# Layer norm of the later tokens with the features on the partitions, in the head of an attention and MLP kernel

## The chip, the cores and the metric

One core of a Trainium2 chip. The metric is the device time of one execution in microseconds (us); several runs are given by their median. Engines: PE is the matrix engine (PEld its weight loads), DVE, ACT and POOL are the vector, scalar and GpSimd engines, SP is SyncE, which issues transfers. Each engine works through its own queue in order and waits on semaphores.

## The reference

2048 tokens of 512 features, float32. The head of the kernel, which is what changes, computes the layer norm and the projections q, k, v.

```
xn = (x - mean(x)) / sqrt(var(x) + 1e-5)              # over the 512 features
q, k, v = split(xn @ wqkv)                            # 32 heads of 16
s = softmax(q k^T / 4) v, heads joined, @ wo
h = relu(xn @ w1 + b1)^2 @ w2 + b2                    # 1792 hidden
out = x + s * silu(h)
```

## The kernel before

Products are made to near float32 accuracy from a high and a low part: every operand `t` is split into `hi` (float32r) and `lo = t - hi`, and a product is three matmuls (hi hi, hi lo, lo hi). With four blocks of 128 features (`KO`) a projection tile of 128 x 512 is twelve matmuls.

**The head**, in program order on PE, ACT, DVE and POOL (`manual_schedule`), works on 16 token tiles of 128 tokens with the tokens on the partitions:
- `load_x` brings a tile, `ln_stats` its mean and variance (DVE) and root (ACT), `ln_norm` scales it (ACT, the first two on DVE).
- `ln_high` turns it on PE: four 128x128 transposes into a `pm` bank of PSUM. ACT copies the bank to the high part of `xTs[c]` (chunk `c` of 512 tokens, features on the partitions), `ln_low` (DVE) subtracts for the low part.
- Between these steps `pump(n)` puts the next `n` projection matmuls into PE's queue: K tiles `("qk", 4, c)`, Q tiles `("qk", 0, c)` and value tiles `("v", c, tt)`. `qk_done` copies a bank to `raw`, POOL splits it into `hl` (`split`) and `qk_store` writes it to DRAM (`q_d`, `k_d`); `v_done` copies a value bank to one of seven `vt` buffers and stores it to `v_d`.
- Weights: `raw_m` and `raw_v` are split into `wa_t` (first Q and K columns, and values). `raw_r`, in the buffer `wv`, is loaded twice, once in the head and once in round 0 of the lead, for the two halves of `wr_t` (the other Q and K columns).
- `spill` writes finished chunks of `xTs` to `xn_d` for the MLP; two more copies keep 256 tokens of chunk 0 in the tile `ka3`; `b1_t` and `b2_t` are loaded.
- When all of K of the first heads is in `k_d`, `load_k` reads it back into two tiles `ka`: twelve transfers of 16 partitions, each a whole row of 2048 keys. `load_q` does the same for Q.

SP's order in the head is left to the scheduler, which places a transfer by its own priorities; from the lead on it is the program's (`lead.enter_context(...)`).

**The lead rounds** follow. Two lanes of 64 rows of PE run side by side; each round a lane issues a matmul of a side tile (the remaining projections, `side_rounds`) and now and then a maximum over 512 keys (`max_mm`, L401 on PE and L408 on DVE), which reads `ka`. Side tiles take the banks `pm`, `pm`, `pd`, `pm`, ... in turn, with three `pm` buffers, and ACT empties a bank when both lanes are done. After the maxima of round group 3 the second half of `wr_t` is split (`split_w`: ACT high parts, POOL low parts):

```
            if g == 0:
                raw_r = [load_w("wv", 3 * P, KO * (5 * P + D))]
            if g == 3:
                for ko in range(KO):
                    split_w(wr_t, ko, slice(3 * P, 6 * P), raw_r[0][:, ko])
```

Lines in the profile: transposes L1394; Q and K tiles of the head L1207, value tiles L1273; side tiles L1303; `raw` and `vt` copies L1224 and L1282; weight copies on ACT L1136; spills L1458; the copies into `ka3` L1538, the biases L1542 and L1545; `load_k` L181, `load_q` L170, weight loads L1145.

Of the kernel before, what the change touches and what calls it, by code (L numbers as in the profile page):

```python
# [73 lines left out]
def kernel(  # L74
    ctx: ExitStack,
    tc: tile.TileContext,
    x: bass.AP,
    wqkv: bass.AP,
# [18 lines left out]
    sp_d = dram.tile([S, D], F32, name="sp_d")  # L97
    xn_d = dram.tile([2, P, KO, S], F32, name="xn_d")
# [33 lines left out]
    with ExitStack() as ph:  # L132
# [42 lines left out]
        def load_k(qd, n):  # L175

            p, j, i = n // 6, n // 3 % 2, n % 3
            if n % 6 == 0:
                kas[qd, p] = ring("ka")
            h = 4 * qd + 2 * p + j  # L180
            nc.sync.dma_start(  # L181
                kas[qd, p][64 * j + DH * i : 64 * j + DH * (i + 1), :].bitcast(F32),
                k_d[h // 8][i % 2, (h % 8) * DH : (h % 8 + 1) * DH, :],
            )
# [13 lines left out]

        def load_q(u, name):
            tiles = []  # L200
            for p in range(2):
                load_q_pair(u, name, p, tiles)
            return tiles
# [928 lines left out]
        def split_w(dst, kos, cols, raw, pool=False):  # L1132
            if pool:
                split((dst[:, 0, kos, cols], dst[:, 1, kos, cols]), raw)
                return
            nc.scalar.activation(dst[:, 0, kos, cols], raw, AF.Copy)  # L1136
            nc.gpsimd.tensor_tensor(
                dst[:, 1, kos, cols], raw, dst[:, 0, kos, cols].bitcast(F32), op=ALU.subtract
            )

        def load_w(name, width, at, kos=(KO,)):
            raw = st.tile([P, KO, width], F32, name=name)
            k0 = 0
            for n in kos:
                nc.sync.dma_start(  # L1145
                    raw[:, k0 : k0 + n],
                    wqkv[:, at + k0 * width : at + (k0 + n) * width].rearrange(
                        "p (k n) -> p k n", n=width
                    ),
                )  # L1150
                k0 += n
            return raw
# [28 lines left out]
        held = []  # L1181
        hold = [True]

        def when_done(fn):
            if hold[0]:
                held.append(fn)
            else:
                fn()

        def let_go():  # L1190
            while held:
                held.pop(0)()

# [8 lines left out]
        def qk_tile(m, c):  # L1202
            ps = qkv_bank()

            for n0, n1 in ((0, 256), (256, 512)) if c == 0 and m % 4 == 0 else ((0, 512),):
                for out_, lh, rh, first_, last_ in qk_terms(m, c, ps):
                    nc.tensor.matmul(  # L1207
                        out_[:, n0:n1], lh(slice(0, P)), rh(slice(0, P))[:, n0:n1],
                        start=first_, stop=last_,
                    )  # L1210
                    if not last_ or n1 < 512:
                        yield
            quick = m % 4 == 0 and not hold[0]

            when_done(lambda: qk_done(m, c, ps, quick, 0))
            yield

        def qk_done(m, c, ps, quick, wait):
            hl = hlp.tile([P, 2, 512], F32R, name="hl")
            if quick:  # L1220
                split_psum(hl[:, 0], hl[:, 1], ps)
            else:
                raw = hlp.tile([P, 512], F32, name="raw", bufs=2)
                nc.scalar.activation(raw, ps, AF.Copy)  # L1224
                split((hl[:, 0], hl[:, 1]), raw)
            later(wait, lambda: qk_store(m, c, hl))
# [27 lines left out]
        def qk_first():  # L1254
            tiles = [qk_tile(m, 0) for m in (4, 0)]
            for _ in range(2):
                for tile_ in tiles:
                    for _ in range(3 * KO):
                        next(tile_)
                        yield  # L1260

# [8 lines left out]
        def v_tile(c, tt):  # L1270
            ps = qkv_bank()
            for out_, lh, rh, first_, last_ in v_terms(c, tt, ps):
                nc.tensor.matmul(out_, lh(slice(0, P)), rh(slice(0, P)), start=first_, stop=last_)  # L1273
                if not last_:
                    yield

            when_done(lambda: v_done(c, tt, ps, 0))
            yield
# [10 lines left out]
        def side_tile(spec, ps, end=None):  # L1289
# [4 lines left out]
            return qk_terms(a, b, ps), end or (lambda: qk_done(a, b, ps, False, 2))  # L1294
# [64 lines left out]
        def load_x(t):  # L1359
            xts[t] = xp.tile([P, D], F32, name="xt", bufs=12)  # L1360
            nc.sync.dma_start(xts[t], xf[t * P : (t + 1) * P, :])
# [5 lines left out]
        def ln_stats(t):  # L1367
# [3 lines left out]
            nc.vector.bn_aggr(mvs[t], stats)  # L1371
            rstds[t] = xp.tile([P, 2], F32, name="rstd", bufs=3)
            nc.scalar.activation(rstds[t][:, 0:1], mvs[t][:, 1:2], AF.Sqrt, bias=eps_t)

        def ln_norm(t):
            rstd = rstds.pop(t)
            xn = xp.tile([P, D], F32, name="xn", bufs=3)
# [3 lines left out]
            )  # L1381
            if t < 2:
                nc.vector.tensor_scalar(
                    xn, xts[t], rstd[:, 0:1], rstd[:, 1:2], op0=ALU.mult, op1=ALU.add
# [146 lines left out]
        while ahead:  # L1531
            pump(1)
# [420 lines left out]
```

## Time and profile before

| | |
|---|---|
| median of 3 runs | 1571.26 us (1571.19 to 1571.65) |
| the profiled execution | 1571.16 us, span 1569.3 us |
| busy share of the span | PE 99%, DVE 86%, ACT 82%, POOL 51% |
| share of the chain that ended last | PE 98% |
| the head | 0 to 62.4 us |

The head ends where PE starts on the first side tile (L1303). The span is what the profile covers of one execution; the chain is followed back from the last instruction to what released each step. DMA share and GB/s of a stretch are over the core's 16 DMA engines. In a timeline row stand the start, the duration of the merged piece, the engine, the line, the operation with its tiles, and the count.

### The profile page before, as it was taken

What the parts mean: (1) busy time and instruction counts of PE and PEld (TensorE: products, weight loads), DVE (VectorE), ACT (ScalarE), POOL (GpSimd) and SP (SyncE); (2) the same over time, 40 slices, a digit from 0 to 9 for tenths busy, and PEclk for the clock granted to TensorE, in tenths of its full rate; (3) what the DMA queues carried; (4) which work ended last, traced back from release to release, by engine and by line L of the source; (5) the groups of instructions that cost most, each with busy time, mean ns of one, the idle gap of its engine ahead of it and who ended that gap; (6) DMA issues with size and microseconds to landing.
All of it is one profiled execution on the core that took longest, in us unless ns stands there. A gap on an engine that the chain in (4) does not pass through costs nothing.

```text
span 1569.3 us, 34206 instructions
## 1 busy us (share of the span) xinstructions
PE 1557.0 (99%) x12364; PEld 872.9 (56%) x12364; DVE 1342.3 (86%) x2307; ACT 1279.3 (82%) x2507; POOL 805.9 (51%) x824
## 2 busy tenths in 40 slices
PE   8999999999999999999999999999999999999998
PEld 7899755555555555555555555555555555555553
DVE  7377899999989998999899999998999999887765
ACT  7222788888889888888898888888888888888886
POOL 6346787348645543354465434545654345654621
PEclk9999999999999999999999999999999999999999
DMA  8967666224544531345244322533552143347665
GB/s 296 255 237 233 198 200 183 51 58 129 173 111 137 148 88 38 77 142 129 73 137 139 71 56 72 157 103 81 145 150 57 37 107 90 75 119 220 205 203 179
DMA packets 152216, 210.11 MB, mean 134 GB/s; under 512 B 58192, under 2 KB 71248, under 8 KB 150480
## 3 DMA queue, kind: packets, MB, share of 16 engines
q1 hardware_dynamic: 151904, 207.67, 46.5%
q8 instruction: 98, 1.61, 0.4%
q14 instruction: 70, 0.57, 0.1%
q10 hardware_dynamic: 144, 0.26, 0.0%
HBM read 141.56 MB, written 63.68 MB: 131 GB/s over the span
## 4 chain that ended last, share of the span: by engine, by line
PE 98%; DVE 1%; DMA 1%; issue 0%; ACT 0%; SPq 0%; DVEq 0%
PE se L487 17%; PE se L1434 12%; PE po L487 9%; PE pd_t L275 8%; PE pm_t L275 8%; PE pm_t L401 7%; PE pm_t L1434 7%; PE se L401 5%; PE pm_t L487 5%; PE pm_t L1303 4%; PE po L1434 4%; PE pd_t L401 2%; PE pm_t L243 2%; PE po L401 1%; PE pd_t L1303 1%; PE se L1273 1%
## 5 line engine op out<-in xcount | busy, mean ns | idle before, releaser
L408 DVE TENSOR_REDUCE mx<-pm_t 128x1 f32<-128x512 f32 x898 | 590.2, 682 | 50.3 <-PE pm_t L401 36.7
L1446 ACT ACTIVATE pt<-se 128x512 f32<-128x512 f32 x983 | 570.5, 623 | 30.4 <-PE pm_t L275 10.2
L408 DVE TENSOR_REDUCE mx<-se 128x1 f32<-128x512 f32 x716 | 478.3, 684 | 90.5 <-PE se L401 62.5
L1434 PE MATMUL se<-qe,ka 64*128 64x512 f32 x1086 | 434.4, 414 | 0.0
L401 PE MATMUL pm_t<-ka,qm 64*128 64x512 f32 x898 | 347.8, 398 | 0.0
L1446 ACT ACTIVATE pt<-pm_t 128x512 f32<-128x512 f32 x546 | 326.9, 622 | 8.9 <-PE pm_t L275 3.9
L1434 PEld LDWEIGHTS se<-qe,ka 64*128 64x128 f32 x1086 | 195.6, 184 | 201.6 <-ACT pt L1446 129.6
L487 PE MATMUL se<-pt,v 128*32 128x512 f32 x2224 | 282.1, 602 | 0.0
L401 PE MATMUL se<-ka,qm 64*128 64x512 f32 x716 | 281.8, 412 | 0.0
L1683 POOL TENSOR_TENSOR sum<-sum,sum 128x512 f32<-128x512 f32 x99 | 127.8, 1291 | 186.3 <-ACT sum L1682 185.9
L1683 POOL TENSOR_TENSOR ot<-ot,sum 128x512 f32<-128x512 f32 x99 | 127.7, 1290 | 180.2 <-ACT sum L1682 180.0
L1434 PE MATMUL pm_t<-qe,ka 64*128 64x512 f32 x575 | 219.0, 407 | 0.0
L275 PE MATMUL pm_t<-w2t,hT 64*128 64x512 f32 x780 | 206.6, 398 | 0.0
L1446 ACT ACTIVATE pt<-po 128x512 f32<-128x512 f32 x299 | 186.7, 625 | 7.8 <-PE pm_t L275 3.8
L401 PEld LDWEIGHTS pm_t<-ka,qm 64*128 64x128 f32 x898 | 164.0, 184 | 35.6 <-DVE mx L408 4.0
L275 PE MATMUL pm_t<-xc,w1s 64*128 64x512 f32 x672 | 177.3, 396 | 0.0
L275 PE MATMUL pd_t<-xc,w1s 64*128 64x512 f32 (+1 forms) x672 | 170.9, 388 | 0.0
L408 DVE TENSOR_REDUCE mx<-pd_t 128x1 f32<-128x512 f32 x233 | 158.7, 681 | 1.5 <-PE pd_t L401 1.5
L408 DVE TENSOR_REDUCE mx<-po 128x1 f32<-128x512 f32 x201 | 137.4, 683 | 22.2 <-PE po L401 18.7
L275 PE MATMUL pd_t<-w2t,hT 64*128 64x512 f32 x564 | 149.3, 397 | 0.0
L401 PEld LDWEIGHTS se<-ka,qm 64*128 64x128 f32 x716 | 131.4, 184 | 21.0 <-DVE mx L408 7.9
L275 PEld LDWEIGHTS pm_t<-w2t,hT 64*128 64x128 f32 x780 | 139.5, 184 | 4.4
(225 smaller groups left out, 2956.9 us busy)
## 6 DMA issues: line engine op xcount, KB each, us to landing
w1s<-w_d SPq DMA_DIRECT2D x84, 256.0 KB
w2t<-w_d SPq DMA_DIRECT2D x42, 512.0 KB
qm<-q_d SPq DMA_DIRECT2D x384, 32.0 KB
ka<-k_d SPq DMA_DIRECT2D x96, 128.0 KB
qe<-q_d SPq DMA_DIRECT2D x384, 32.0 KB
q_d<-hl SPq DMA_DIRECT2D x16, 512.0 KB
g<-g_d SPq DMA_DIRECT2D x32, 256.0 KB
k_d<-hl SPq DMA_DIRECT2D x15, 512.0 KB
```

The lines of the kernel that those rows point to most:

```text
L243: mm = nc.tensor.matmul(out_() if callable(out_) else out_, lh(r), rh(r), start=first_ and lane == 0, stop=last_ and lane == 1, skip_group ...
L275: mm = nc.tensor.matmul(out_() if callable(out_) else out_, lh(r), rh(r), start=first_ and lane == 0, stop=last_ and lane == 1, skip_group ...
L401: nc.tensor.matmul(ps, qms[u][p][64 * j : 64 * j + 64, qb * P : (qb + 1) * P], kas[qd, p][64 * j : 64 * j + 64, kc * 512 : (kc + 1) * 512] ...
L408: return nc.vector.tensor_reduce(mxs[u][:, c, kc : kc + 1], ps, axis=AX.X, op=ALU.max)
L487: nc.tensor.matmul(po[32 * j : 32 * j + 32, :], vs[qd][:, (4 * kb + j) * VW : (4 * kb + j) * VW + 32], pts[j], start=first, stop=last, ski ...
L1273: nc.tensor.matmul(out_, lh(slice(0, P)), rh(slice(0, P)), start=first_, stop=last_)
L1303: mm = nc.tensor.matmul(out_, lh(r), rh(r), start=first_ and lane == first, stop=last_ and lane != first, skip_group_check=True,)
L1434: nc.tensor.matmul(se, kas[qd, j // 2][b : b + 64, kb * P : (kb + 1) * P], qes[u][j // 2][b : b + 64, :], start=True, stop=True,)
L1446: return nc.scalar.activation(pts[j], se, AF.Exp, scale=0.25)
L1683: nc.gpsimd.tensor_tensor(pos["sum"], pos["sum"], part, op=ALU.add)
```

## The change

Tokens 0 to 1023 are normalised as before, with `ln_norm` in place and its steps written out one by one. Tokens 1024 to 2047 (chunks 2 and 3) are read twice: once as rows (`load_rows`, two tokens to a partition, 512 KB a group of 256 tokens), for the statistics only, and once as columns from a second input `xc`, the same tokens laid out with the features on the partitions (`load_columns`, 512 KB a group; the layout is made on the host). Means and roots of a chunk go out to DRAM and come back broadcast to all partitions (`row_out`, `row_in`, issued by ACT; 512 KB each way back). DVE then subtracts and multiplies (`column_norm`), ACT writes the high part, DVE the low part. The columns lie in the buffers `wv`, `wm` and one of their own. There are no transposes for these tokens.

The order of the head's matmuls by tile is kept, and every step of the head is now written out, SP's transfers too: `lead.enter_context(tc.manual_schedule(engines={SP}))` stands at the start of the head. The high part of the value weights moves from POOL to ACT. K is read back in pieces: chunks 0 and 1 in twelve transfers during the head, chunk 2 in twelve more behind the last K tile, and chunk 3 in twelve straight from `hl` (`move_k`), without DRAM; SP issues all. The first spills, the copies into `ka3`, the biases and the last stores come behind these.

```
+        def move_k(n, eng):
+            p, j, i = n // 6, n // 3 % 2, n % 3
+            h = DH * (2 * p + j)
+            eng.dma_start(
+                kas[0, p][64 * j + DH * i : 64 * j + DH * (i + 1), 3 * 512 :].bitcast(F32),
+                outs["qk", 4, 3][0][h : h + DH, i % 2].bitcast(F32),
+            )
...
+        def row_out(c):
+            nc.scalar.dma_start(st_d[c], moments[c])
+
+        def row_in(c):
+            spread[c] = xp.tile([P, P, 2, 2, 2], F32, name="sb", bufs=2)
+            nc.scalar.dma_start(
+                spread[c].rearrange("p a h s j -> p (a h s j)"),
+                st_d[c].rearrange("a h s j -> (a h s j)")[None, :].to_broadcast([P, 1024]),
+            )
+
+        def column_norm(g, i):
+            c, h = divmod(g + 2, 2)
+            v = columns[g].rearrange("p k (a j) -> p k a j", j=2)
+            nc.vector.tensor_tensor(
+                v, v, spread[c][:, None, :, h, i, :].to_broadcast([P, KO, P, 2]),
+                op=(ALU.subtract, ALU.mult)[i],
+            )
...
+        matmuls(("v", 0, 3), 12)
+        row_in(3)
+        for i in range(2):
+            column_norm(2, i)
+        copy_out(("v", 0, 3))
+        store(("v", 0, 3))
+        column_high(2)
+        matmuls(("qk", 0, 1), 12)
+        for i in range(2):
+            column_norm(3, i)
+        column_low(2, nc.vector)
+        column_high(3)
+        column_low(3, nc.vector)
+        for p in range(2):
+            load_q_pair(0, "qm", p, qms[0])
+        copy_out(("qk", 0, 1))
+        split_out(("qk", 0, 1))
+        matmuls(("v", 1, 0), 12)
+        for i in range(2):
+            column_norm(4, i)
+        for n in range(12):
+            load_k(0, n, 0, 2)
...
+        matmuls(("qk", 4, 2), 12)
+        copy_out(("qk", 4, 2))
+        split_out(("qk", 4, 2))
+        store(("qk", 4, 2))
+        matmuls(("v", 1, 2), 12)
+        copy_out(("v", 1, 2))
+        matmuls(("qk", 4, 3), 12)
+        copy_out(("qk", 4, 3), True)
+        split_out(("qk", 4, 3), True)
+        for p in range(2):
+            for n in range(6):
+                move_k(6 * p + n, nc.sync)
+            for n in range(6):
+                load_k(0, 6 * p + n, 2, 3)
+        store(("qk", 4, 3))
+        store(("v", 1, 2))
+        for c in range(2):
+            for k in range(2):
+                spill(c, k)
+        for ko in range(KO):
+            args = wr_t, slice(ko, ko + 1), slice(0, 3 * P), raw_r
+            high_w(*args)
+            low_w(*args)
         lx.close()
...
         for k in range(2):
+            keep_first(k)
+        load_bias()
         fill_ring("qm", 2, 0.0)
...
+        matmuls(("v", 1, 3), 12)
+        copy_out(("v", 1, 3))
+        store(("v", 1, 3))
+        matmuls(("qk", 0, 2), 12)
+        copy_out(("qk", 0, 2))
+        split_out(("qk", 0, 2))
+        store(("qk", 0, 2))
+        matmuls(("v", 2, 0), 12)
+        copy_out(("v", 2, 0))
+        store(("v", 2, 0))
...
             if g == 0:
-                raw_r = [load_w("wv", 3 * P, KO * (5 * P + D))]
+                raw_r = w_tile("wv", 3 * P)
+                load_w(raw_r, KO * (5 * P + D), 0, KO)
             if g == 3:
                 for ko in range(KO):
-                    split_w(wr_t, ko, slice(3 * P, 6 * P), raw_r[0][:, ko])
+                    high_w(wr_t, slice(ko, ko + 1), slice(3 * P, 6 * P), raw_r)
+                    low_w(wr_t, slice(ko, ko + 1), slice(3 * P, 6 * P), raw_r)
```

More of the change, by code (lines that the diff above doesn't have):

```diff
@@ L97 @@
     sp_d = dram.tile([S, D], F32, name="sp_d")
+    st_d = {c: dram.tile([P, 2, 2, 2], F32, name=f"st_d{c}") for c in (2, 3)}
     xn_d = dram.tile([2, P, KO, S], F32, name="xn_d")
@@ L1200, in qkv_bank, with qk_done @@
             return pd.tile([P, 512], F32, name="pd_t")
[L1202 to L1218, printed above, removed]
-            hl = hlp.tile([P, 2, 512], F32R, name="hl")
[L1220 to L1225, printed above, removed]
+        def qk_done(m, c, ps, wait):
+            hl = hlp.tile([P, 2, 512], F32R, name="hl")
+            raw = hlp.tile([P, 512], F32, name="raw", bufs=2)
+            nc.scalar.activation(raw, ps, AF.Copy)
+            split((hl[:, 0], hl[:, 1]), raw)
             later(wait, lambda: qk_store(m, c, hl))
@@ L1404, in ln_low, with load_rows @@
             )
[L1406 to L1418 removed]
+        rows, moments, columns, spread, wide = {}, {}, {}, {}, []
+        def load_rows(g):
+            rows[g] = xp.tile([P, 2, D], F32, name="xg", bufs=2)
+            nc.sync.dma_start(
+                rows[g], xf[512 + g * 256 : 768 + g * 256, :].rearrange("(p j) d -> p j d", j=2)
+            )
```

448 lines of the change are left out of this document (279 added, 169 removed).

## The prediction

> **What bounds the kernel now.** I read the page first, then the chain that ended last, then the timeline of each queue over the first 90 us.
>
> ```profile
> PE 1557.0 (99%) x12364; PEld 872.9 (56%) x12364; DVE 1342.3 (86%) x2307; ACT 1279.3 (82%) x2507; POOL 805.9 (51%) x824
> ...
> PE 98%; DVE 1%; DMA 1%; issue 0%; ACT 0%; SPq 0%; DVEq 0%
> ```
>
> PE carries 98% of the chain, so time taken out of PE's queue shows at the end, and so does any new hole in it. The change touches only the head (0 to 62 us) and, through the queues, the first 25 us of the lead rounds. The chain there:
>
> ```profile
> 19.37 2.31 PE se L1273 x10
> 21.69 0.44 PE pm_t L1394 x4
> ...
> 23.75 0.44 PE pm_t L1394 x4
> ...
> 36.81 0.43 PE pm_t L1394 x4
> ...
> 59.62 2.80 PE pd_t L1273 x12
> 62.43 0.43 PE pm_t L1303
> ```
>
> In this stretch PE never waits. A projection tile is twelve matmuls, 2.80 us; the four transposes of a token tile are 0.44 us. The rows at 23.75 and 36.81 are the first and the last of the eight token tiles from 1024 on; the lead starts at 62.4.
>
> **What goes.** Eight token tiles lose their transposes: 8 x 0.44 = 3.5 us off the path. The sixteen projection tiles stay, so with nothing else the lead would start at 62.4 - 3.5 = 58.9. That is the ceiling of the gain. The ACT and DVE work of those tiles goes too; it was hidden, 0.
>
> **Columns on DVE.** Four groups of 256 tokens, each with three tensor operations on 128x1024 (subtract, multiply, low part) that the trace does not have. The nearest rows (calls; shortest, median and longest in ns):
>
> ```profile
> L993 DVE TENSOR_TENSOR rb<-rb,tsm x2: 425/426/426, 1513.8 to 1515.6; 128x256 f32<-128x256 f32 x2
> L958 DVE TENSOR_TENSOR g<-g,s x12: 650/692/1233, 1514.7 to 1554.8; 128x512 f32<-128x512 f32 x12
> L117 POOL TENSOR_TENSOR hl<-raw,hl x5: 1287/1292/1297, 21.5 to 82.8; 128x512 fp32r<-128x512 f32 x5
> ```
>
> 0.425 for 256 elements and 0.692 for 512: by the same slope 1.23 us for 1024 (ends: 0.69, as if the size were free, and 1.38, twice 0.692); I take 1.23, twelve are 14.8 us. When they can start follows from the transfers (stretch, PE, PEld, DVE, ACT, POOL busy, clock, DMA share, GB/s; and one token load of 256 KB with nothing before it):
>
> ```profile
> 66.00:70.00 4.00, 4.00 (x38) 3.20 (x36) 3.67 (x7) 0.00 (x0) 0.00 (x0) 1.00 1.05 403
> 64.00:82.00 18.00, 18.00 (x157) 15.96 (x155) 14.91 (x25) 4.61 (x10) 3.82 (x4) 1.00 0.97 346
> 52.00:62.00 10.00, 10.00 (x44) 8.07 (x43) 0.69 (x1) 1.80 (x3) 5.01 (x5) 1.00 1.06 136
> ```
>
> ```profile
> 0.74 2.67 DMA xt<-in_A_x_dram
> ```
>
> 256 KB at 375 GB/s is 0.7 us, so a transfer has about 2.0 us besides. The last rows can be asked for when DVE has read the first ones, near 22 us; 2 MB at 346 GB/s bring them near 28, their statistics go out and come back spread over the partitions in two transfers of about 2 us, the first group's earlier. DVE starts on the columns near 33 and ends near 48. PE wants chunk 3 for its K tile at 19.37 + 10 x 2.80 + 0.44 = 47.8. I take 0.7 us late (ends 0 and 4, below).
>
> **K rows on SyncE.** K of chunk 3 ends at 47.8 + 0.7 + 2.8 = 51.3. About 1 us later its two parts are copied out (an estimate: a DVE step of 0.69 as in the L958 row, and the first part beside PE's end), so the rows are ready near 52.3. Then SyncE issues 24 row transfers where 12 stood, and its whole queue is in program order. What an issue takes, over nine K rows:
>
> ```profile
> 50.81 4.00 SPq L181 DMA_DIRECT2D ka<-k_d  x9
> ```
>
> 0.44 us; 24 are 10.7. The first six that read chunk 2 back must wait for its store, 1 us by my count: SyncE is through at 64.0. What PE needs of it: the third block of 512 keys, which the second lane asks for first at
>
> ```profile
> 64.34 0.39 PE L401 MATMUL se<-ka,qm 64*128 64x512 f32 x1
> ```
>
> 1.9 us behind the start of the lead, so at 61.5. Twelve rows are issued by 58.6 and land by 60.6: hidden, 0, but with 1 us of room (other end 1.5).
>
> **What stands behind the K rows.** This is the term that decides. In program order SyncE next issues the store of K chunk 3, one value store, the four spills of chunks 0 and 1, two copies into ka3, both biases, two value stores and a Q store, and only then, in round 0 of the lead, the second load into wv (the other half of the weights wr_t). Before, the scheduler had put the first spills at 19 us, and the load came here:
>
> ```profile
> 19.38 1.32 SPq L1458 DMA_DIRECT2D xn_d<-xT  x2
> ...
> 67.97 1.15 SPq L1145 DMA_DIRECT2D wv<-in_A_wqkv_dram  x1
> ```
>
> Its reader on ACT came at 77.5, with room to spare:
>
> ```profile
> 77.04 0.60 ACT L1282 ACTIVATE vt<-pd_t 128x512 f32<-128x512 f32 x1 [2.65 <-PE pd_t L1303]
> 77.53 1.75 ACT L1136 ACTIVATE wr_t<-wv 128x384 fp32r<-128x384 f32 x4
> 80.24 0.60 ACT L1224 ACTIVATE raw<-pm_t 128x512 f32<-128x512 f32 x1 [0.96 <-PE pm_t L1303]
> ```
>
> ACT runs in program order. Behind the four weight copies stands the copy of the side tile (qk, 0, 3), which frees a pm bank; the fourth side tile after it takes that bank, and PE, in order too, stands still until then. That side tile begins with the second of these matmuls,
>
> ```profile
> 84.71 0.57 PE L1303 MATMUL pm_t<-wa_t,xT 64*128 64x512 f32 x2
> ```
>
> at 84.9. If the load lands at T, PE passes there at T + 1.75 + 0.6 + 0.1 = T + 2.45. T up to 82.4 is no loss against before; only T up to 79.6 keeps a gain of 2.8 (3.5 less the 0.7 of the columns). (The four value-weight copies that ACT takes over from POOL earlier in the head are of the same kind, 1.75 us together if nothing hid them; PE's queue is full beside them, 0.)
>
> T by bytes, from the sizes of one issue each:
>
> ```profile
> xn_d<-xT SPq DMA_DIRECT2D x6, 1024.0 KB
> v_d<-vt SPq DMA_DIRECT2D x16, 272.0 KB
> ...
> k_d<-hl SPq DMA_DIRECT2D x6, 512.0 KB
> ...
> wv<-in_A_wqkv_dram SPq DMA_DIRECT2D x2, 768.0 KB
> ...
> xn_d<-xT SPq DMA_DIRECT2D x2, 512.0 KB
> ka<-xT SPq DMA_DIRECT2D x2, 512.0 KB
> ```
>
> Spills 2 x 512 + 2 x 1024, copies 2 x 512, a K and a Q store 2 x 512, value stores 3 x 272, the second bias 256 (2 KB to each partition), the load 768: 6960 KB, 7.13 MB. The 136 GB/s of 52 to 62 us belong to K rows, sixteen partitions at a time; these transfers are of the kind that runs at 346 to 403, and I take 375: 19.0 us (17.7 to 20.6). T = 64.0 + 0.4 + 19.0 + 2.0 = 85.4, PE passes at 87.9 instead of 84.9: +3.0. PE has then stood from 84.9 - 2.8 = 82.1, 5.8 us, and after its idle start this trace has slow matmuls:
>
> ```profile
> 8.98 2.60 PE L1207 MATMUL se<-xT,wa_t 128*128 128x256 f32 x10 [0.84 <-ACT xT L1396]
> ...
> 16.79 1.91 PE L1207 MATMUL se<-xT,wa_t 128*128 128x256 f32 x14
> ```
>
> Ten in 2.60 us where fourteen take 1.91: 1.2 us lost on ten. I add 1.3 (ends 0 and 2.6).
>
> **Sum.** +3.0 + 1.3 = +4.3. The head's own gain is inside it, since the wait ends at a fixed time. The profiled execution took 1571.16 us, 0.1 under the median: 1571.2 + 4.3 = 1575.5.
>
> The Trainium skill ("TensorE: Matmul & The Clock Gate", Part 1) says that PE drops to half clock after an idle window of about 3.4 us and needs as long a busy one to come back; by it that last term would be 1.7 and the sum 1575.9. The trace agrees in kind with the two rows, but its granted clock reads 1.00 in every stretch shown, so no row here shows the gate itself.
>
> **Rivals.** (1) Faster: the backlog drains in time, T up to 79.6, so SyncE is through by 60 and 400 GB/s hold. For it: 403 held for 4 us, and with rows ready at 51.5, no wait for the store and 403 throughout, T is 51.5 + 10.7 + 0.4 + 17.7 + 2.0 = 82.3, no longer far. Against it: a whole stretch of 18 us ran at 346. It gives 1567.7 to 1568.4. (2) About even: T between 80 and 84, the loss eats the gain and PE stands under 4 us: 1568.5 to 1573. (3) Columns late as well: one L958 call, with two SBUF inputs, took 1.233 us where others take 0.650. If DVE and POOL hold each other up in such calls, two splits of POOL between 33 and 48 us (1.29 each for the low part alone) push chunk 3, the K rows and T by 2.6 to 4 us: 1578 to 1579.5. The Trainium skill ("SBUF — State Buffer", SBUF: two separate sides) has just this rule, an exclusive lock on a shared pair of ports; the 1.233 fits it, and no row of the head can show it, where DVE's second operand came from PSUM. (4) That the change doesn't do its part can be left out: the 32 transposes are gone from the program.
>
> **How the numbers follow.** Late load by itself 0.48; late columns too 0.14; even 0.24; gain kept 0.14. The likeliest gives 1575.5, its own range 1573 to 1578. The range over the cases is 1569 to 1580. About 0.2% (3.1 us) is what a measurement of this kernel can tell from no change: slower (over 1574.4) is 0.6, late columns and most of the late load; faster (under 1568.1) 0.1, the better part of the kept gain; the rest, 0.3, lies within.
>
> **What would show it.** Right: no transposes after the eighth token tile; the lead's first matmul at 59 to 60; SyncE without a break from 52 past 70 and the wv load near 75; ACT standing before its second four weight copies, released by a DMA, until 84 to 88; behind it a hole of 4 to 7 us in PE, and the same intervals as before after that. Wrong: the four weight copies at their place near 74 (the end is then near 1568); a hole at the K tile of chunk 3 (rival 3); a hole at the first maxima (K rows late).

## The result and the profile after

The changed kernel takes 1587.29 us (median of 4 runs, 1587.01 to 1587.31) against 1571.39 for the kernel before, beside it on the same chip: ratio 1.0101, 95% interval 1.0083 to 1.0118. It is slower by 15.9 us. The profiled execution took 1587.31 us, span 1585.5.

The page first: PE's busy time is what it was (1557.0 before), its share of the chain fell from 98 to 93%. PE has no more to do, it stands still.

```profile
PE 1558.2 (98%) x12332; PEld 866.7 (55%) x12332; DVE 1349.1 (85%) x2295; ACT 1274.0 (80%) x2493; POOL 808.8 (51%) x824
...
PE 93%; DMA 0%; ACT 0%; DVE 0%; SPq 0%; issue 0%; DVEq 0%
```

Where: the first exponential of the attention comes at 135.63 before and at 151.08 after, 15.45 later; behind it little is added (the two spans differ by 16.2). One row of ACT's timeline, before and then after:

```profile
135.63 0.59 ACT L1446 ACTIVATE pt<-se 128x512 f32<-128x512 f32 x1
```
```profile
151.08 0.59 ACT L1513 ACTIVATE pt<-se 128x512 f32<-128x512 f32 x1
```

Next SyncE's timeline from the last K tile on (start, duration of the merged piece, line, tiles, count). L1286 are the moves out of the split tile, L184 the reads from DRAM, L1525 the spills, L1530 the copies into `ka3`, L1536 and L1539 the biases, L1134 the load of `wv`:

```profile
55.09 0.37 SPq L1158 DMA_DIRECT2D k_d<-hl  x1
56.75 4.55 SPq L1286 DMA_DIRECT2D ka<-hl  x6
62.47 2.65 SPq L184 DMA_DIRECT2D ka<-k_d  x6
65.17 3.67 SPq L1286 DMA_DIRECT2D ka<-hl  x6
68.88 2.90 SPq L184 DMA_DIRECT2D ka<-k_d  x6
...
72.80 4.91 SPq L1525 DMA_DIRECT2D xn_d<-xT  x4
77.81 2.87 SPq L1530 DMA_DIRECT2D ka<-xT  x2
80.72 1.43 SPq L1536 DMA_DIRECT2D b_t<-in_B_b_dram  x1
82.20 5.17 SPq L1539 DMA_DIRECT2D b_t<-in_B_b_dram  x1
...
88.92 1.46 SPq L1134 DMA_DIRECT2D wv<-in_A_wqkv_dram  x1
```

SyncE is through the K rows at 71.8 and comes to the weights at 88.9 (68.0 before). What waits for them, on ACT and then on PE; the brackets hold the idle time and its releaser:

```profile
96.15 1.76 ACT L1142 ACTIVATE wr_t<-wv 128x384 fp32r<-128x384 f32 x4 [16.08 <-DMA wv<-in_A_wqkv_dram]
97.82 0.57 ACT L1188 ACTIVATE raw<-pm_t 128x512 f32<-128x512 f32 x1
```
```profile
64.38 0.50 PE L1314 MATMUL pm_t<-wa_t,xT 64*128 64x512 f32 x1
...
98.45 2.93 PE L1314 MATMUL pm_t<-wa_t,xT 64*128 64x512 f32 x12 [10.68 <-ACT raw L1188]
```

The weights land at 96.1, and PE passes the matmul that waits for the bank (it begins the fourth side tile behind the one that ACT has to copy) at 98.45 instead of 84.9. That is 13.55 of the 15.45 us. Behind the hole PE is slow for some microseconds. The columns below are stretch, busy time (and count) of PE, PEld, DVE, ACT and POOL, granted clock, DMA share, GB/s:

```profile
88.00:98.00 10.00, 0.00 (x0) 0.00 (x0) 0.90 (x2) 1.85 (x5) 1.25 (x2) 0.74 0.99 331
98.00:104.00 6.00, 5.55 (x30) 4.44 (x32) 1.29 (x2) 1.49 (x3) 4.50 (x5) 0.58 0.85 327
```

A mean clock of 0.58 over the 5.55 busy us of the second stretch loses some 2.3 us (an estimate), about the rest.

The lead started at 64.38 instead of 62.36, although 3.5 us of transposes are gone. The cause is the columns on DVE (L1468 subtract and multiply, L1482 low part) and, beside them, a split on POOL:

```profile
36.09 2.54 DVE L1468 TENSOR_TENSOR wv<-wv,sb 128x1024 f32<-128x1024 f32 x2 [3.05 <-DMA st_d<-mvg]
39.76 2.49 DVE L1468 TENSOR_TENSOR wv<-wv,sb 128x1024 f32<-128x1024 f32 x2 [1.13 <-ACT xT L1475]
...
44.56 3.88 DVE L1468 TENSOR_TENSOR wm<-wm,sb 128x1024 f32<-128x1024 f32 x2
...
51.98 1.23 DVE L1482 TENSOR_TENSOR xT<-xc,xT 128x1024 fp32r<-128x1024 f32 x1
```
```profile
45.20 2.15 POOL L119 TENSOR_TENSOR hl<-raw,hl 128x512 fp32r<-128x512 f32 x1
```

They begin at 36.1. ACT sent the moments (means and roots) out at 23.91 and stood 5.19 us until they had landed:

```profile
30.10 0.60 ACT L1254 ACTIVATE vt<-se 128x512 f32<-128x512 f32 x1 [5.19 <-DMA st_d<-mvg]
```

The way back, asked for at 29.73, took up to 6.4 more. (The first DVE row names the second chunk's way out as its releaser; by the program the operation waits for `sb`, the way back.) At the end of the chain ACT, in program order, copies the columns before it empties a bank, and PE stands for that bank:

```profile
50.90 1.06 ACT L1475 ACTIVATE xT<-xc 128x1024 fp32r<-128x1024 f32 x1 [1.35 <-DVE xc L1468]
51.86 0.58 ACT L1254 ACTIVATE vt<-se 128x512 f32<-128x512 f32 x1
```
```profile
52.49 0.49 PE L1238 MATMUL se<-xT,wa_t 128*128 128x512 f32 x1 [2.20 <-ACT vt L1254]
```

So the K tile of chunk 3 starts at 52.5, behind a hole of 2.20: 4.7 us after the 47.8 at which PE could have taken it. The tiles do not quite keep their old order either: the K tiles of chunks 2 and 3 now stand behind more value tiles and a Q tile. Before, K of chunk 3 was the first half of this row of PE, and its store went out at 45.3:

```profile
39.87 5.76 PE L1207 MATMUL se<-xT,wa_t 128*128 128x512 f32 x24
```

So the K rows, which left from 50.81 on before, would leave later in the new order even without a wait.

### The profile page after: what moved, and what is told of

It reads as the page before. It is cut to its first block, busy times and chain, and to the rows that moved or that the text cites. A ratio compares the mean times of both kernels' runs of the same rounds, so it can differ in the third digit from the quotient of the medians.

```text
span 1585.5 us, 34142 instructions
## 1 busy us (share of the span) xinstructions
PE 1558.2 (98%) x12332; PEld 866.7 (55%) x12332; DVE 1349.1 (85%) x2295; ACT 1274.0 (80%) x2493; POOL 808.8 (51%) x824
## 4 chain that ended last, share of the span: by engine, by line
PE 93%; DMA 0%; ACT 0%; DVE 0%; SPq 0%; issue 0%; DVEq 0%
PE se L484 17%; PE se L1501 12%; PE po L484 9%; PE pm_t L272 8%; PE pm_t L398 7%; PE pd_t L272 7%; PE pm_t L1501 7%; PE se L398 5%; PE pm_t L484 5%; PE po L1501 4%; PE pm_t L1314 3%; PE pd_t L398 2%; PE pm_t L240 1%; PE po L398 1%; PE pd_t L240 1%; PE pd_t L1314 1%
## 5 line engine op out<-in xcount | busy, mean ns | idle before, releaser
L398 PE MATMUL se<-ka,qm 64*128 64x512 f32 x716 | 271.0, 412 | 0.1
L1501 PEld LDWEIGHTS pm_t<-qe,ka 64*128 64x128 f32 x575 | 103.1, 184 | 68.8 <-ACT pt L1513 44.7
```

The lines of the kernel that those rows point to most:

```text
L398: nc.tensor.matmul(ps, qms[u][p][64 * j : 64 * j + 64, qb * P : (qb + 1) * P], kas[qd, p][64 * j : 64 * j + 64, kc * 512 : (kc + 1) * 512] ...
L1501: nc.tensor.matmul(se, kas[qd, j // 2][b : b + 64, kb * P : (kb + 1) * P], qes[u][j // 2][b : b + 64, :], start=True, stop=True,)
```

## The experiments

Theory A: two chains are late, SyncE's single order behind the 24 K rows (the hole at 87) and the columns in the head (the lead 2 us later instead of 3.5 earlier), and they are the whole loss. Theory B: the bytes themselves stall the lead wherever they stand.

**The weight load first behind the K rows.**
```
+        for ko in range(KO):
+            args = wr_t, slice(ko, ko + 1), slice(0, 3 * P), raw_r
+            high_w(*args)
+            low_w(*args)
+        raw_r = w_tile("wv", 3 * P)
+        load_w(raw_r, KO * (5 * P + D), 0, KO)
         store(("qk", 4, 3))
         store(("v", 1, 2))
         for c in range(2):
...
             if g == 0:
-                raw_r = w_tile("wv", 3 * P)
-                load_w(raw_r, KO * (5 * P + D), 0, KO)
```


> The changed kernel with one move: the second load into wv is issued right behind the 24 K rows, ahead of the stores, spills, copies and biases (the same transfers, another order on SyncE). Theory A (the place of this load in SyncE's order makes the loss): it is issued near 72 and lands near 76, ACT's four weight copies come at their place near 80, the 10.7 us hole of PE at 87.5 is gone and the clock stays at 1.00; what is left is the late start of the lead (64.4 against 62.4), so 1573.4 us, 1572.5 to 1574.5. Rival B (the backlog itself, 24 row transfers and 3 MB more, makes the loss, and the load is only the first to meet it): something else behind it is late, a value buffer, an hl buffer or a bank, and a hole of several us opens elsewhere in the lead: 1580 us or more. Rival C (the columns make it): 1585 or more.

1579.97 us, ratio 1.0052 (1.0037 to 1.0067): almost half of the loss is gone. ACT's weight copies stand at 79.58 and the hole at 87 is gone. A new one stands at 115, on the Q rows of unit 1 (the next load into `qm`), which SyncE reaches at 106.07 (91.64 in the kernel before) because the spills, the biases (8.5 us of issuing here) and the stores now stand between:

```profile
106.07 6.27 SPq L172 DMA_DIRECT2D qm<-q_d  x6
```
```profile
114.89 0.76 PE L398 MATMUL se<-ka,qm 64*128 64x512 f32 x1 [3.56 <-DMA qm<-q_d]
```

So A names the hole at 87, but its 1573.4 is missed and B is half right: moving one transfer ahead makes the next one late.

**Two spills behind the load** (chunk 1's, 1 MB each; the load stays in round 0).
```
-        for c in range(2):
-            for k in range(2):
-                spill(c, k)
+        for k in range(2):
+            spill(0, k)
...
                 load_w(raw_r, KO * (5 * P + D), 0, KO)
+                for k in range(2):
+                    spill(1, k)
```

> The changed kernel with the two spills of chunk 1 (1 MB each) issued behind the second load into wv instead of ahead of it. Theory A, as a dose: the load lands 2 MB / 0.35 MB per us = 6 us earlier, at 90 instead of 96.1, PE's hole shrinks from 10.7 to about 5 us, and the time falls by 6 us to 1581.4 (1579.5 to 1582.5, the lower the less the clock falls). Rival B or C: the time stays within 2 us of 1587.3.

1582.6 us, ratio 1.0072 (1.0055 to 1.0088).

```profile
90.66 1.76 ACT L1142 ACTIVATE wr_t<-wv 128x384 fp32r<-128x384 f32 x4 [9.76 <-DMA wv<-in_A_wqkv_dram]
```

The weights land 5.5 us earlier for 2.1 MB less ahead of them, 380 GB/s. The dose is right; 4.7 us of it reached the end. (In this profiled execution the head lost more as well: behind its hole of 2.20 eleven matmuls took 3.99 instead of 2.82, and the lead started at 65.63.)

**Columns 2 and 3 loaded behind the store of v0.**
```
         load_rows(4)
-        load_columns(2)
-        load_columns(3)
...
         store(v0)
+        load_columns(2)
+        load_columns(3)
         store(v1)
```

> The changed kernel with the loads of the columns 2 and 3 (1 MB) issued behind the first three stores instead of ahead of the moments' way out and back. Theory D (the moments' way through DRAM took 5.8 and 6.3 us because it queued behind that megabyte and the stores on the DMA engines): the way out takes about 3 us, DVE starts on the columns at 32 to 33 instead of 36.1, the two holes of PE at 42.7 and 50.2 shrink, the K rows and with them the second load into wv come 3 to 4 us earlier: 1583.5 us (1582.5 to 1585). Rival (5 to 6 us are what such a small transfer with its wait takes): DVE starts at 36, 1587.

1588.26 us, ratio 1.0106 (1.0091 to 1.0122): a miss, no different from the changed kernel. The first way out took 3.8 us instead of 5.8, but now the columns and the second way out (29.80 to 36.98) wait in the same traffic, and DVE begins at 37.65.

**SyncE's order in the head left to the scheduler**, as before the change.
```
-        lead = ExitStack()
-        lead.enter_context(tc.manual_schedule(engines={mybir.EngineType.SP}))
         raw_m = w_tile("wm", 2 * P)
...
+        lead = ExitStack()
+        lead.enter_context(tc.manual_schedule(engines={mybir.EngineType.SP}))
         made = [0, 0]
```

> The changed kernel with SyncE's order in the head left to the scheduler again, as before the change; columns, K rows in pieces and all else stay. Theory A: spills and biases go out early, in the gaps, the second load into wv comes before 75, there is no hole at the fourth later side tile: 1571 to 1575 us. Rival B or C: the hole or another of its size stays: 1583 or more.

1578.27 us, ratio 1.0044 (1.0029 to 1.0059). It issued the spills of chunk 0 and the second bias by 19 us, the weights at 80.53. The hole is 1.74 and the twelve matmuls behind it take 1.65 instead of 2.93, so no clock is lost there:

```profile
90.86 1.65 PE L1314 MATMUL pm_t<-wa_t,xT 64*128 64x512 f32 x12 [1.74 <-ACT raw L1188]
```

The time is over the 1571 to 1575 of A because the head is later still: the lead starts at 66.26. Behind a hole of 1.41 that ends at 44.8 and one of 0.32 the clock is slow (0.58 and 0.56 granted from 46 to 50), and eleven matmuls take 4.38 instead of 2.82:

```profile
45.64 4.38 PE L1238 MATMUL se<-xT,wa_t 128*128 128x512 f32 x11 [0.32 <-DVE xT L1482]
```

**Spills and biases ahead of the first K rows, the weights first behind the last.**
```
+        for c in range(2):
+            for k in range(2):
+                spill(c, k)
+        load_bias()
         for n in range(12):
             load_k(0, n, 0, 2)
...
+        raw_r = w_tile("wv", 3 * P)
+        load_w(raw_r, KO * (5 * P + D), 0, KO)
         for k in range(2):
             keep_first(k)
```

> The four spills of chunks 0 and 1 and the two bias loads are issued ahead of the first K rows (where the DMA engines were 39% busy), and the second load of the wv weights stands right behind the 24 K rows, ahead of the two copies into the ka ring and of every lead store. Theory A (SyncE's one order with some 7 MB behind the K rows is the whole of the hole at 87 us; the late head is worth 2 us): the weights land near 80, no hole of over 1 us near 87 and none near 115, where the run with the load alone first had one of 3.56; lead start 64.4 as in the changed kernel; 1573.4 us (1572.5 to 1575). Theory B (the same bytes stall the lead wherever they stand): a hole of 3 us or more elsewhere between 64 and 125 and 1578 or more. A third possibility: SyncE's order is now 4 us fuller ahead of the K rows, they come later, and the maxima wait for them between 64 and 80: 1576 to 1580.

1586.31 us, ratio 1.0095 (1.0078 to 1.0112): nothing won. The six transfers (four spills, two biases) took SyncE 9.3 us; the *first* load of `wv` slid from 52.58 to 62.98, ACT's first weight copies stand ahead of a bank copy, and PE stood there:

```profile
62.98 0.75 SPq L1134 DMA_DIRECT2D wv<-in_A_wqkv_dram  x1
```
```profile
71.61 3.78 PE L1238 MATMUL pd_t<-wa_t,xT 128*128 128x512 f32 x8 [8.45 <-ACT vt L1254]
```

**Blocks three and four of K read from DRAM in 12 rows instead of 24.**
```
-        for p in range(2):
-            for n in range(6):
-                move_k(6 * p + n, nc.sync)
-            for n in range(6):
-                load_k(0, 6 * p + n, 2, 3)
         store(("qk", 4, 3))
+        for n in range(12):
+            load_k(0, n, 2, 4)
```

> The 24 short K rows (12 moves out of the split tile, 12 reads of the third block) become 12 reads of blocks three and four together from k_d, behind the store of that tile, as the kernel before read its K rows; nothing else moves. Theory A (SyncE's issue order sets when the second wv load lands): the store goes out at 57, lands near 59.5, 12 x 0.44 = 5.3, SyncE is through at 65 instead of 71.8, the weights land near 89 instead of 96.1, the hole shrinks from 10.7 to some 4 us: 1579 (1577.5 to 1581). Rival (the DMA engines' drain sets it, SyncE's issue time being hidden): the weights land at 94 or later and 1584 or more. Another: the last block of keys now makes its way through DRAM and comes too late for the first maxima: a hole between 64 and 72 on the K tiles.

1584.44 us, ratio 1.0083 (1.0068 to 1.0098). SyncE waits until 63.84 for the store of chunk 3 (landed some 4.6 us after the last store was issued) and is through at 69.5, 2.2 earlier; the weights land 2.4 earlier, at 93.7. The landing follows SyncE, nearly one for one, as A has it. The time is not A's 1579, since the wait for the store paid back most of the halved count. The other possibility on record came too, if small: PE stood 0.73 us at 68.8 for K rows.

**Column groups in other buffers** (2 and 3 in those loaded early, 4 and 5 in the wide one).
```
-            if g == 2:
+            if g == 4:
                 wide.append(w_tile("wv", D))
-            if g < 4:
-                columns[g] = wide[0][:, :, (g - 2) * 256 : (g - 1) * 256]
-            elif g == 4:
+            if g > 3:
+                columns[g] = wide[0][:, :, (g - 4) * 256 : (g - 3) * 256]
+            elif g == 3:
                 columns[g] = w_tile("wm", 2 * P)
...
         store(v0)
+        load_columns(4)
+        load_columns(5)
```


> The column groups change buffers: groups 2 and 3, needed first, take the two buffers that are loaded early (the start and 14 us), groups 4 and 5 take the shared wide tile and are loaded behind the store of v0. Theory (the head is late because the moments' way out and back, 5.8 and 6.3 us, lies behind 1 MB of columns, and because the norm of group 3 waits for the copy of group 2): the first column operation on DVE at 30 to 32 instead of 36.1, no PE hole over 0.5 us between 40 and 54, lead start 60.5 (60 to 61.5) instead of 64.4; the weights' landing moves with SyncE's order by 3 to 4 us, so the hole stays near 10: 1583.4 (1582 to 1585). Rival 1 (SyncE issues without a gap from 38 to 55, so nothing behind it moves): lead start 60.5 too, but the hole grows to 14 and the time stays at 1587. Rival 2 (the columns' own DVE chain, not the round trip, is late): holes of over 1 us on the copies stay between 42 and 54, lead start 63 or later, 1587.

1586.62 us, ratio 1.0099 (1.0084 to 1.0114). DVE begins at 33.54, not 31, and the hole at 44 is gone; the one before chunk 3 stays (2.17 at 50.46), and this time eleven matmuls behind it take 4.39 instead of 2.82. Lead start 64.03. The chain itself, not only its start, is late: rival 2. SyncE is through at 70.2, the weights land at 95.5.

**Early traffic and swapped columns together.** The edit joins the one that moved spills and biases ahead of the K rows and the last one.

> The two edits before this one together: spills and biases early, wv load first behind the K rows, and the column groups swapped. If both causes are as stated and do not overlap: lead start 60.5, no hole over 1 us up to 125, 1569.5 us (1568.5 to 1571), about 2 us below the kernel before, which is what 8 transposes less give with no new wait. If the SyncE order now binds the earlier lead (K rows or weights late by the 4 us that the lead comes earlier): 1573, as the run with the traffic alone.

1586.01 us, ratio 1.0093 (1.0078 to 1.0109): the hole of the early traffic again, 10.14 at 71.4.

**Both chains, with the spills and biases in other places.** Besides the swapped columns:
```
         ln_low(3)
+        for k in range(2):
+            spill(0, k)
+        load_bias()
...
         store(v1)
+        load_columns(4)
+        load_columns(5)
+        for p in range(2):
+            load_q_pair(0, "qm", p, qms[0])
...
             load_k(0, n, 0, 2)
+        for k in range(2):
+            spill(1, k)
...
+        raw_r = w_tile("wv", 3 * P)
+        load_w(raw_r, KO * (5 * P + D), 0, KO)
         store(("qk", 4, 3))
```

> Both chains mended without filling SyncE's list ahead of the K rows: chunk 0's spills and the biases at 18 us, where SyncE is idle; the 12 Q rows in its idle stretch 30 to 34; chunk 1's spills behind the first 12 K rows; the second wv load first behind the 24 K rows; the column groups swapped as in the run before, groups 4 and 5 loaded behind the store of v1, so that the way back of the moments (6.3 us) does not run beside them. Theory A (the two late chains are all): first column operation on DVE at 31, no PE hole over 0.5 us from 40 to 125, lead start 60.5 (60 to 61.5), SyncE through the K rows at 66 to 67, weights landed by 72: 1569.5 us (1568.5 to 1571), 1.8 below the kernel before. Theory C (the change has a third cost, not yet seen, such as the K tiles, the wr_t copies or the clock): lead start 60.5 to 62, but 1572 or more, with a hole whose releaser names it.

1582.31 us, ratio 1.0073 (1.0058 to 1.0088). No hole near 87 or 115, but the first wv load, issued at 55.43 behind the spills of chunk 1, lands at 65.7:

```profile
68.04 4.78 PE L1238 MATMUL pd_t<-wa_t,xT 128*128 128x512 f32 x12 [6.40 <-ACT vt L1254]
```

**The head's part of that alone:** the swapped columns and the second of those four pieces.

> The head's part of the run with all: the column groups swapped, 4 and 5 loaded behind the store of v1, the 12 Q rows in SyncE's idle stretch; spills, biases and the second wv load as in the changed kernel. Theory A: lead start 60.5; SyncE, issue-bound from 31 on, is through the K rows at 65 to 66 instead of 71.8; the weights land 24.3 later, near 90, PE passes at 92 and the hole at 84 is 7 to 8 us: 1580 (1578 to 1582). If the lead start stays at 63 or later, the columns' DVE chain, not its start, is what holds PE, and the time is 1582 to 1585.

1586.44 us, ratio 1.0098 (1.0082 to 1.0115). The columns begin at 33.98, but the hole of 2.21 stays, the clock is halved behind it and the lead starts at 64.66; SyncE is through at 70.5, the weights land at 95.7 and not near 90. So the head gained nothing here, and what a gain in it would be worth is not shown by this run.

**The queue's part alone:** the first and the last of those pieces, the columns as in the changed kernel, chunk 1's spills behind the weights.

> The queue's part alone: chunk 0's spills and the biases at 18 us, the second wv load first behind the 24 K rows, everything else as in the changed kernel. Theory A: the weights land near 76, no hole near 87; SyncE is through its list near 84 and issues unit 1's Q rows near 94, so none near 115 either; lead start 64.4 stays: 1573.4 us (1572.5 to 1575). Theory B (some transfer behind the K rows is late whatever stands first): a hole of over 2 us between 85 and 120, 1577 or more.

1576.13 us, ratio 1.0031 (1.0020 to 1.0042). No hole behind the start of the lead. What is left is the head's: holes of 1.53, 2.17 and 2.11 us and a lead that starts at 67.08, so the time is over A's 1575. The first hole is put down to the rows that now stand behind the biases; no run tests that.

**The queue again, the biases at the end of the lead:** the first experiment with
```
-        load_bias()
         fill_ring("qm", 2, 0.0)
...
             if g == 18:
                 load_v(0)
+            if g == 22:
+                load_bias()
```

> The run with the wv load ahead of the rest, and the two bias loads (8.5 us of SyncE there) moved to the end of the lead; the head untouched. Theory A: lead start 64.4 as in the changed kernel, weights near 79, unit 1's Q rows issued by 97 instead of 106, so neither of the two long holes (87, 115): what is left is the head's delay, 2.0 us: 1573.4 us (1572.5 to 1574.5). If a hole of over 1 us stays between 85 and 120, the backlog itself is too long, biases or not: 1575 or more.

1574.98 us, ratio 1.0023 (1.0014 to 1.0032). Up to 52.6 its head is that of the changed kernel, hole for hole. Then (PE, the changed kernel first, then this one):

```profile
53.27 2.82 PE L1238 MATMUL se<-xT,wa_t 128*128 128x512 f32 x11 [0.28 <-DVE xT L1482]
```
```profile
53.38 4.37 PE L1238 MATMUL se<-xT,wa_t 128*128 128x512 f32 x11 [0.28 <-DVE xT L1482]
```
```profile
54.00:56.00 2.00, 2.00 (x6) 0.50 1.04 234
```

Behind the same hole of 2.2 us the clock stays full in one execution and is halved in the other (last row: stretch, its length, busy PE, clock, DMA share, GB/s): 1.55 us more. With that taken off, the profiled execution (1574.98) would be at the 1573.4 that A gave.

**POOL's split of the Q tile of chunk 1 moved away from the columns.**
```
         copy_out(("qk", 0, 1))
-        split_out(("qk", 0, 1))
...
-        store(("qk", 0, 1))
...
         store(("qk", 4, 2))
+        split_out(("qk", 0, 1))
+        store(("qk", 0, 1))
```

> Only POOL's split of the Q tile of chunk 1 and its store are moved, behind those of the K tile of chunk 2; everything else is as in the changed kernel. Theory (POOL's split and DVE's two-input column operations slow each other): the DVE pair that took 3.88 takes 2.5, the xT tile of chunk 3 is ready at 51.8 instead of 53.2, the hole of 2.20 at 52.5 shrinks to 0.8 and the lead starts at 63.0; the hole at 87 grows by as much and the time stays at 1587. Rival (that pair is slow for another reason, its tile coming late by DMA, say): 3.88 stays and the lead starts at 64.4.

1586.8 us in a single run. On DVE:

```profile
44.39 2.49 DVE L1468 TENSOR_TENSOR wm<-wm,sb 128x1024 f32<-128x1024 f32 x2
```

3.88 became 2.49; the hole of 2.20 became 0.80 and the lead starts at 63.6. The two engines do hold each other up, for 1.4 us of the head. The hole at 87 grows from 10.68 to 11.45, so the end hardly moves: a gain in the head is worth little while that hole ends at a time that SyncE sets.

**Both chains, second version:** the last two edits, the swapped columns, and
```
-        fill_ring("ka", 1, -1.0)
         for n in range(2):
             fill_ring("qm", n, 0.0)
+        fill_ring("ka", 1, -1.0)
...
         store(first_q)
+        for p in range(2):
+            load_q_pair(0, "qm", p, qms[0])
+        load_columns(4)
+        load_columns(5)
         store(v0)
```

> A second version with both chains mended. Head: column groups swapped; the qm fill goes ahead of the ka fill on POOL, so that the 12 Q rows (small transfers) leave SyncE from 29 on and the 1 MB of columns 4 and 5 and the stores of v0 and v1 follow them, which clears the stretch in which the moments go out and come back; POOL's split of the Q tile of chunk 1 stands behind the split of the K tile of chunk 2, so that it does not run beside the columns on DVE. Queue: second wv load first behind the 24 K rows, spills behind it, biases only at the end of the lead. Theory A: first column operation at 30 to 31, the DVE chain of 12 x 1.23 plus one wait of 1.1 ends near 47, no PE hole over 0.5 us before 125, granted clock 1.00 throughout, lead start 60.0 to 60.5: 1569.3 us (1568.5 to 1570.5), 2 us below the kernel before. Theory C (a third cost): the holes are gone and the time is still 1571 or more. If the moments still come back at 33 or later, lead start 61 to 62.5 and 1570.5 to 1572.

1575.22 us, ratio 1.0025 (1.0015 to 1.0035). The moments came back at 32.6, but now columns 4 and 5 were late, 2.17 on DVE; a hole of 2.68 before chunk 3, a halved clock behind it (4.78 for twelve matmuls), lead start 64.08.

**Columns 4 and 5 between the Q rows, the split of K of chunk 1 ahead of the `ka` fill.** Against the version above:
```
+        load_q_pair(0, "qm", 0, qms[0])
         load_columns(4)
         load_columns(5)
+        load_q_pair(0, "qm", 1, qms[0])
...
         split_out(("qk", 4, 1))
+        fill_ring("ka", 1, -1.0)
...
         copy_out(("v", 1, 0))
+        matmuls(("v", 1, 1), 12)
+        copy_out(("v", 1, 1))
         column_high(4)
```

> The last version with one point changed in the head: columns 4 and 5 are issued between the two halves of the 12 Q rows, 3.5 us earlier, so DVE's wait of 2.17 for them goes; POOL's split of the K tile of chunk 1 goes ahead of the ka fill, so that it does not run beside the first column pair; the copy of v(1,1)'s bank stands ahead of the column copies on ACT. Theory A (the head's holes and the loss of clock behind them are all that is left): first column operation at 32.6, the chain ends near 48.5, the PE hole at 51 shrinks from 2.68 to under 0.7, the granted clock stays at 1.00, lead start 60.4 to 61: 1570.2 us (1569 to 1571.2), 1 to 2 below the kernel before. Theory C (something else is left): lead start under 61.5 and 1572 or more, or a new hole at the K tiles between 60 and 70 because the lead now comes earlier than its K rows.

1571.94 us (11 runs, 1570.93 to 1574.49), ratio 1.0005 (0.9996 to 1.0014): no change from the kernel before. So mending the two chains takes back the whole loss of 15.9 us. It does not bring the gain: the 3.5 us of the transposes are still missing, and the time is over the 1569 to 1571.2 that A gave.

```profile
49.50 2.82 PE L1238 MATMUL se<-xT,wa_t 128*128 128x512 f32 x11 [0.72 <-DVE xT L1482]
...
58.79 3.07 PE L1238 MATMUL pd_t<-wa_t,xT 128*128 128x512 f32 x12 [0.90 <-ACT vt L1254]
61.78 0.50 PE L1314 MATMUL pm_t<-wa_t,xT 64*128 64x512 f32 x1
```

The lead starts 0.6 us before that of the kernel before, not 3.5, with two holes left. The profiled execution is still 0.5 us ahead at 1195 us and 0.2 ahead at its last vector operation, and 0.5 behind at the end, when only the last stores are under way; no run here gives the cause of that.

**The causes of those two holes moved as well.**
```
+        copy_out(("qk", 4, 1))
+        split_out(("qk", 4, 1))
         row_root(3)
...
         column_high(4)
+        copy_out(("v", 1, 1))
...
         copy_out(("v", 1, 3))
+        for ko in range(KO):
+            args = wr_t, slice(ko, ko + 1), slice(0, 3 * P), raw_r
+            high_w(*args)
+            low_w(*args)
```

> The last version with the causes of its two remaining PE holes (0.72 at 49.5 on the xT tile of chunk 3, 0.90 at 58.8 on a bank) moved: the copy of the K tile of chunk 1 goes ahead of the second root on ACT, so that POOL's split of it ends before DVE's first column pair; the copy of column group 4 goes ahead of that of v(1,1)'s bank; the wr_t copies stand behind the copy of v(1,3)'s bank instead of ahead of it. Theory A (the eight transposes are the change's gain, 3.5 us of PE in which no order of the others gets lost): no hole over 0.3 us from 40 to 125, lead start 60.2 to 60.6, 1569.7 us (1569 to 1570.6), ratio 0.9985 to 0.9995 to the kernel before. Rival: the lead, starting earlier than its K rows and Q rows allow, waits for them and the time stays at 1571 to 1572.

1572.66 us (11 runs, 1571.63 to 1574.95), ratio 1.0007 (0.9998 to 1.0016): nothing won again, near the 1571 to 1572 of the rival. The lead starts at 60.08, and then

```profile
64.62 0.47 PE L398 MATMUL se<-ka,qm 64*128 64x512 f32 x1 [2.18 <-DMA ka<-k_d]
```

with a clock of 0.72 from 64 to 68. This is the slowest of its runs, so the row shows the kind of loss, not its mean. In this execution the gain of the transposes meets the next limit, the third block of K rows, which SyncE issues from 59.38 on. That the other runs lose theirs at the same place is not shown.

## Why the prediction was wrong

The direction, the place and the mechanism were as stated: the second load of `wv`, ACT's copies behind it, the bank of the fourth side tile, PE's hole, a slow clock after it; PE passed at the landing + 2.3 (forecast 2.45). It went wrong in size: +4.3 forecast, +15.9 measured, and 1587.3 is outside the range. The step that failed is the time at which SyncE is through the K rows, 71.8 instead of 64.0; the bytes behind it were the smaller part. By its steps:

- *Columns on DVE.* One operation of 1024 takes 1.22 to 1.28 where POOL is not beside it, as taken from the slope (1.23). The start, 33, was 36.1: a transfer was priced at 2.0 us, from a load with nothing before it, and the two ways through DRAM took 5.8 and up to 6.4 in the traffic of columns and stores. The end, 48, was 53.2: besides the start, 1.1 for the shared wide tile and 1.4 for POOL. Instead of 0.7 late the K tile of chunk 3 was 4.7 late (52.5 against 47.8), beyond the upper end of 4. The hole there was the sign named for rival 3, but the delay fed the same late load, and 1579.5 was that rival's limit. The lead came at 64.4 instead of the 59 to 60 that would have shown the forecast right.
- *K rows.* Ready at 56.75, not 52.3 (+4.45, the head's delay). The 24 issues took 13.8 instead of 10.7 (0.57 each in the mean; the first six moves alone took 4.55), the wait for the store of chunk 2 1.2 as forecast 1. SyncE was through at 71.8, not 64.0: **this term failed**, by 7.8.
- *What stands behind.* 24.4 us instead of 21.4: the rate was 324 to 331 GB/s (72.8 to 96 and 88 to 98 us), not 375, and below the range taken (346 to 403).
- So T was 96.1 instead of 85.4 (+10.7). The clock added about 2 instead of 1.3. 4.3 + 10.7 + 0.7 is 15.7.
- *First maxima.* They did not wait for the K rows, as forecast, but the lead was late. With the lead at 60.08, in the last run, PE stood for them until 64.62, where the prediction had them landed by 60.6 with 1 us of room.

The range was too narrow in two ways. The late ends (3.3 more for the columns, 1.6 for the bytes, 1.3 for the clock) were not added up, though a chain in one queue adds all its delays with the same sign; and even their sum gives only 1581.7, for the issue of the K rows had no late end at all, and the columns and the rate fell outside theirs. The rule on two-input operations of DVE beside POOL ("SBUF — State Buffer", SBUF: two separate sides, of the Trainium skill) was held to a side case of 0.14. The 3.88 against 2.49 shows the slowing, though not that a lock makes it, and it should have stood in the sum.

Left open: why the same hole of 2.2 us halves the clock in one execution and not in the other. Among the profiled executions whose head has a hole of 2.16 to 2.21 us there, seven show slow matmuls behind it and three do not. The Trainium skill ("TensorE: Matmul & The Clock Gate", Part 1) says that the activity window of about 3.4 us runs freely, so that the effect varies from run to run. The rows of the head agree with that, but they lose clock behind holes shorter than the window, and no run here shows the window.

## What to carry to other kernels

When an engine's order is written out by hand, list what stands behind each wait in every queue, the issuing engine above all, and find the first reader of each transfer: here one weight load behind 24 row transfers and 7 MB cost 13.5 us, while taking 3.5 us of matrix work away gained nothing. Putting one transfer first only moves the lateness to the next; what helped was sending what nobody reads soon (spills, biases) behind everything that is read. A small round trip through DRAM on a critical chain is priced at its loaded time, not at its empty one.

## What the hardware showed that was not expected

- A 4 KB write and a 512 KB broadcast read through DRAM took 5.8 and up to 6.4 us beside columns and stores; the write took 3.8 when the columns were issued behind it.
- The load of the second bias, 256 KB broadcast to 128 partitions, held SyncE for 5.26 us at 22 (kernel before), 5.17 at 82 (changed kernel), 4.05 at 50 (spills and biases early) and 0.65 at 19 (SyncE's order left to the scheduler). What makes the difference is not shown.
- The granted clock was 0.58 (98 to 104 us) behind a hole of 10.68 us, 0.50 (116 to 120 us, weights first) behind one of 3.56, and either 1.00 or 0.50 behind 2.2. It was 1.00 behind one of 1.74 but 0.58 behind one of 1.41 followed by one of 0.32, so the length of the hole alone does not tell it.
